# A retention layer and an MLP on one core: where the decay of the queries is multiplied in

## The chip, the cores and the metric

The kernel runs on one core of a Trainium2 chip. TensorE (PE) multiplies matrices and writes PSUM; VectorE (DVE) and ScalarE (ACT) empty PSUM, cast and combine; GpSimd (POOL) and SyncE (SP) issue transfers here. The metric is the device time of one execution in microseconds (us), lower is better.

## The reference

A retention layer (attention without softmax, with a decay per head) over batch 8, 8 heads, 576 positions, head size 64, and then a two-matrix MLP with a leaky rectifier on the 4608 tokens of 512 features. Cut to what matters:

```python
scores = (1 / sqrt(64)) * q @ k.T
gamma = 1 - 2 ** (-5 - arange(8))                 # one per head
Dmat = where(i >= j, gamma ** (i - j), 0)         # position i looks back at j
x = ((scores * Dmat) @ v), heads side by side     # 4608 x 512
h = x @ w_in                                      # w_in 512 x 2048
out = maximum(0.01 * h, h) @ w_out                # w_out 2048 x 512
```

`gamma ** (i - j)` splits into a factor of the query's position and one of the key's position. The kernel multiplies v by the key's factor.

## The kernel before, in words

**Units and groups.** The tokens are cut into 36 units u of 128 rows, each two chunks of 64 positions of one sequence (a sequence is 9 chunks, so some units span two). Four units make one group g of 512 tokens for the MLP; there are nine groups. Decays are counted inside blocks of 256 positions, four chunks; `place(c)` is a chunk's number in its block, 0 to 3.

**Jobs of a unit** (names as in the lists of orders):

- `ld u.1`, `ld u.0`, `ld u.2` load k, q and v in float32 (line 346). Units 0 to 11 come through POOL's queue (k0 and q0 through SP's), later ones through SP for k and q and POOL for v. Each of the three has four buffers, so the load of unit u waits for the cast of unit u - 4.
- `ck u`, `cq u`, `cv u` write 16-bit copies. `ck` is a plain cast (line 371). `cq` multiplies q by the query's factor and the scale, `cv` multiplies v by the key's factor; on VectorE that is one product with a table from the constants `cs` (line 375), on ScalarE eight small ones, one per head (line 381).
- `tp u.x` and `yt u.x` transpose k and q on TensorE and copy the result out of PSUM (units 0 to 7); `tr u` does it by one transposing transfer on SP's queue (from unit 8).
- `sb u` sums k and v into the running state (PSUM `sc`), `st u.j` adds it to the state kept in float32 on VectorE, `sx` casts that state to 16 bits. At a block's end `st` also multiplies by gamma to the 256th.
- `ca u` (or `sa u` in the first four units) multiplies k with q in PSUM `sc`, `mk u` applies the causal mask on VectorE, `ow u` (or `oa u`) multiplies by v and adds the state's part in PSUM `ot`.
- `x u` copies `ot` to the 16-bit tile `xT` (line 591), which the MLP reads. `ot` has two slots, so `ow` of unit u + 2 waits for `x u`.

**The MLP.** For groups 0 and 1 the first layer is plain: `h g.f.t` are blocks of matmuls of feature tiles from f on and tokens from t on, `l ...` the rectifier on ScalarE. The blocks of group 0 are cut by unit where that lets them start early: `h0.4.0` and `h0.6.0` need x0 and x1, `h0.4.256` needs x2, `h0.4.384` needs x3, and `h0.8.0` to `h0.15.0` need all four. `wi0` to `wi3` load the four quarters of w_in, `wo0` to `wo3` those of w_out. From group 2 on the first layer (`a g.n`), and in all groups the second (`b g`), is a scheme of seven products in place of eight: products p1 to p7 on TensorE (four matmuls of 256 columns in `a`, two halves of eight in `b`), copies `cA`, `u2`, `k5` out of PSUM on either engine, sums `22` and `12` on VectorE, results `11` and `21`. `xs` and `m` are the sums of its operands on VectorE; `wm` and `ws` are those of the weights, made once.

**The order.** Nothing is scheduled by a tool at build time: one list, `ORDER`, names every job, and each engine runs its own in that list's order; an engine whose next job has to wait holds all that stand behind it. `ENGINE` says which of VectorE and ScalarE runs a job that both can do. `+n@p` puts n idle matmuls of 512 columns (fillers) on TensorE; `@p` names one of four PSUM banks (`acc`). The beginning of TensorE's part of the list before:

```
+13 tp1.0 tp0.0 tp0.1 sb0 +4 tp1.1 sa0 +3 sb1 tp2.1 +2 sa1 tp2.0 oa0 +7 sa2 sb2 oa1 +2 tp3.1 h0.6.0 +2
tp3.0 h0.4.0 sa3 oa2 sb3 tp4.1 h0.4.256 oa3 tp4.0 tp5.0 h0.11.0 h0.9.0 h0.10.0 tp5.1 ca4 sb4 h0.4.384
```

Of the kernel before, what the change touches and what calls it, by code (L numbers as in the profile page):

```python
# [33 lines left out]
class Plan:  # L34
# [52 lines left out]
    for eng, names in {  # L87
        "DVE": """
            ck0 cq0 sx0.0 yt0.0 cq1 sx0.1 cv1 cq2 sx1.0 yt2.1 ck3 cq3 yt3.1 cv3 sx2.1 yt3.0 cq4 cv4 x3 ck5 cq5
            cv5 yt5.1 cq6 sx5 cv6 cq7 ck7 cv7 yt7.0 b0.cA cv8 ck10 sx8.0 cv9 cq9 cq11 cq12 cv10 b1.cA cv13 ck15  # L90
            cv14 cq14 cv15 cq15 sx13.1 sx14 cq16 cv16 cv17 cq17 cq18 a2.3.k5 sx17.0 cv18 sx18 cq19 a3.1.u2 x17
            cv20 ck21 cq21 sx19 a3.2.k5 cq22 cv22 sx20 ck23 cv23 cq23 x20 cv24 cq25 sx23 a4.2.cA cv25 a4.2.u2
            cq26 cq27 cv27 sx25 a5.0.u2 a5.0.k5 cq28 cq29 cv29 ck30 cq30 cv30 ck31 cv31 cq32 sx30 cq33 ck33
            a6.0.cA cv33 cv34 ck34 cq35 cq34 a6.2.cA b5.u2 cv35 a6.3.u2 x32 a7.0.cA x33 a7.0.k5 b5.21 a7.1.cA
            b6.11 b6.u2 a7.3.cA a7.3.u2 a8.0.k5 b7.k5 a8.2.u2 a8.2.k5 b7.21 a8.3.u2 b8.21
        """,
        "ACT": """
            cv0 yt0.1 x0 ck1 ck2 yt1.1 yt1.0 cv2 yt2.0 x1 sx1.1 sx2.0 x2 sx3.0 ck4 sx3.1 yt4.1 yt4.0 ck6 sx4.1
            x4 yt5.0 x5 yt6.0 yt6.1 sx6 yt7.1 sx7 x7 x6 ck8 b0.11 cq8 ck9 b0.u2 cq10 b0.k5 cv11 ck12 sx9 x8 ck11
            cv12 sx10 cq13 b0.21 x9 ck13 sx11 b1.11 sx12 x10 b1.u2 x11 ck14 a2.0.cA b1.k5 a2.0.u2 a2.0.k5 x12  # L100
            a2.1.cA a2.1.u2 x13 a2.1.k5 ck16 ck17 sx15 a2.2.cA a2.2.u2 b1.21 a2.2.k5 sx16 x14 a2.3.cA x15
            a2.3.u2 ck18 b2.cA a3.0.cA b2.11 a3.0.u2 a3.0.k5 a3.1.cA cv19 b2.u2 x16 a3.1.k5 ck19 b2.k5 a3.2.cA
            ck20 cq20 a3.2.u2 cv21 b2.21 ck22 x18 a3.3.cA a3.3.u2 a3.3.k5 x19 b3.cA a4.0.cA b3.11 sx21 ck24
            a4.0.u2 a4.0.k5 cq24 a4.1.cA a4.1.u2 sx22.1 a4.1.k5 x21 b3.u2 ck25 b3.k5 ck26 sx24 a4.2.k5 x22 cv26
            a4.3.cA x23 a4.3.u2 a4.3.k5 ck27 b3.21 a5.0.cA b4.cA ck28 cv28 sx26.0 b4.11 x24 ck29 a5.1.cA a5.1.u2
            a5.1.k5 x25 sx27 sx28 b4.u2 a5.2.cA x26 sx29 b4.k5 a5.2.u2 a5.2.k5 x27 a5.3.cA ck32 a5.3.u2 cv32
            a5.3.k5 cq31 b4.21 x28 x29 sx31.1 a6.0.u2 a6.0.k5 sx32 b5.cA a6.1.cA b5.11 a6.1.u2 x30 a6.1.k5 x31
            a6.2.u2 a6.2.k5 sx33 b5.k5 ck35 a6.3.cA a6.3.k5 sx34 sx35.0 a7.0.u2 b6.cA a7.1.u2 a7.1.k5 a7.2.cA
            a7.2.u2 b6.k5 a7.2.k5 x34 x35 a7.3.k5 a8.0.cA b6.21 a8.0.u2 b7.cA b7.11 a8.1.cA b7.u2 a8.1.k5
            a8.1.u2 a8.2.cA a8.3.cA a8.3.k5 b8.cA b8.u2 b8.k5 b8.11x so8.11x b8.11y  # L110
# [6 lines left out]
    ld0.1 ld0.2 ld0.0 ld1.0 ld1.1 ld2.1 ck0 ld2.0 cq0 ld1.2 cv0 cq1 ld2.2 +13@3 tp1.0@0 wi1 tp0.0@1 tp0.1@2 sb0 +4@3  # L117
    yt0.1 ld3.1 st0.0 ck1 yt0.0 ld3.0 cq2 yt1.0 tp1.1@3 ck2 sa0 +3@1 cv1 ld4.1 yt1.1 st0.1 sx0.0 sb1 tp2.1@2 +2@0
    mk0 ld3.2 sx0.1 cv2 sa1 tp2.0@1 ld4.0 st1.0 oa0 +7@0 mk1 sx1.0 st1.1s x0 yt2.1 yt2.0 sx1.1 sa2 sb2 oa1 +2@0
    ld5.0 x1 ck3 wi2 st2.0 tp3.1@0 mk2 h0.6.0@3 +2@1 ld4.2 st2.1 ck4 cq3 l0.6.0 yt3.1 tp3.0@2 ld5.1 sx2.0 h0.4.0@1  # L120
    yt3.0 cv3 ld5.2 sa3 oa2 cq4 sb3 wi3 x2 tp4.1@3 st3.0 mk3 l0.4.0 wi0 h0.4.256@0 sx3.0 sx2.1 cq5 ld6.0 oa3
    l0.4.256 tp4.0@2 x3 tp5.0@1 yt4.0 st3.1s ld6.1 h0.11.0@0 sx3.1 yt5.0 ld6.2 h0.9.0@2 yt4.1 ck5 cv4 ld7.0
    h0.10.0@1 l0.9.0 tp5.1@3 ld7.2 l0.10.0 ca4 sb4 h0.4.384@2 mk4 ld7.1 cv5 h0.8.0@1 l0.4.384 st4.1 ld8.2 yt5.1 ow4
    sb5 x4 h0.15.0@2 st5.0 sx4.1 st5.1 l0.11.0 h0.14.0@3 sx5 ld8.1 ca5 l0.14.0 cq6 l0.8.0 ld9.2 ws3.1 h0.13.0@0 mk5
    ld9.1 h0.0.128@3 l0.13.0 cv6 wo2 h0.0.384@1 l0.0.128 ld10.2 l0.15.0 tp6.0@0 h0.0.256@3 ck6 yt6.0 ld10.1 tp6.1@2
    l0.0.384 ow5 sb6 wo0 x5 h0.12.0@0 st6.0s yt6.1 ld8.0 h1.0.0@1 cv7 l0.0.256 cq7 ld9.0 h1.2.0@2 l1.0.0 ck7 st6.1
    ld10.0 tp7.0@3 h1.8.0@1 yt7.0 wo1 m0.0.0 h1.12.0@3 l1.8.0 ws3.0 sx6 ck8 ca6 sb7 l1.12.0 ld11.2 h0.0.0@1 st7.0
    l1.2.0 cv8 ck9 h1.4.0@3 mk6 ld12.2 l0.12.0 st7.1 h1.14.0@2 l0.0.0 cv9 wo3 l1.4.0 m0.1.0 tp7.1@0 sx7 sb8 h1.6.0@1
    st8.0s yt7.1 ow6 ca7 h1.10.0@3 ld11.1 x6 mk7 l1.14.0 wm2.0 ow7 sb9 ld13.2 m0.2.0 x7 b0.p1.0@0 l1.6.0 wm0.0
    h1.12.256@2 l1.10.0 cv10 ld11.0 wm1.0 h1.2.256@1 m0.0.1 h1.8.256@3 l1.2.256 m0.1.1 ld14.2 l1.12.256 h1.14.256@1  # L130
    sx8.0 l1.8.256 st9.0 ck10 b0.p1.1 l1.14.256 ws1.1 cq8 m0.2.1 h1.10.256@2 b0.cA@3 h1.0.256@1 ws1.0 b0.p6.0 st9.1
    l1.0.256 wm2.1 l1.10.256 h1.4.256@1 wm0.1 sx9 tr8 ld12.1 b0.p5.0@2 wm1.1 ld12.0 m0.3.1 b0.p5.1 cq9 b0.p6.1 ws2.1
    b0.k5 m0.3.0 b0.p2.0 b0.u2 cv11 sb10 ca8 b0.p7.0 mk8 tr9 ld13.1 st10.0 b0.p3.0 ck11 st10.1s ld15.2 cq10 ld13.0
    b0.p7.1 cq11 b0.p3.1 b0.22 b0.p2.1 l1.4.256 b0.12 wm3.0 ow8 ca9 sb11 wm3.1 cv12 b0.p4.0 tr10 ws4.1 b0.p4.1 mk9
    tr11 st11.0 ck12 b1.p1.0@1 ld16.2 ws2.0 ck13 st11.1 b1.p1.1 x8 m1.0.0 b0.21 h1.6.256@2 cq12 sx10 so0.1 b1.cA@3
    ow9 l1.6.256 ca10 ws4.0 sb12 sx11 b1.p2.0 m1.1.0 x9 tr12 ld14.0 st12.0 b1.p2.1 cq13 mk10 ld14.1 st12.1s b1.p6.0
    ld15.1 m1.0.1 ow10 b0.11 ca11 m1.2.0 a2.0.p1.0@2 b1.11 so0.0 b1.p5.0@0 m1.1.1 a2.0.cA@1 cv13 x10 b1.p5.1 mk11
    sx12 ld17.2 b1.p6.1 m1.2.1 m1.3.0 ow11 b1.u2 sb13 ca12 m1.3.1 a2.0.p2.0 x11 b1.p7.0 tr13 ld15.0 a2.0.11 xs2.0
    cq14 b1.k5 ld16.0 a2.0.p5.0@2 st13.1 b1.p7.1 a2.0.k5 xs2.1 ld17.0 mk12 a2.0.p6.0 xs2.2 b1.p3.0 a2.0.u2 sx13.1
    ck15 ck14 ld16.1 xs2.3 a2.0.p7.0 a2.0.p3.0 a2.0.22 b1.p3.1 a2.0.12 l2.0.22 a2.0.p4.0 b1.22 l2.0.12 a2.1.p1.0@2  # L140
    cv14 a2.0.21 b1.p4.0 b1.12 ld18.2 a2.1.p5.0@1 cq15 sb14 a2.1.k5 ow12 ca13 tr14 a2.1.cA@0 b1.p4.1 st14.0 x12
# [910 lines left out]
```

## Time and profile before

| what | value |
|---|---|
| median of 3 runs | 279.2 us (279.14 to 279.57) |
| profiled execution, its time | 279.54 us |
| its span, first to last instruction | 277.7 us |
| POOL busy | 72.4 us (26% of the span) |
| HBM read, written | 36.81 MB, 9.44 MB: 167 GB/s over the span |

The profile is one execution. Its page gives for each engine the busy time, its share of the span and the number of instructions; PEld is TensorE's weight load, which overlaps its matmuls. Rows of tenths cut the span into 40 slices of about 7 us. A row of waits reads: who waited, for whom, microseconds in total, how often, the longest. A row of the timeline reads: start, length, engine, line, operation, out<-in, shape, count, and in brackets how long the engine was idle before it and what ended that. A row of the groups by line reads: line, engine, operation, out<-in, shapes, count | busy us, mean ns of one | idle us before them and what ended it. A row of a window reads: from:to, length, then busy us of PE, PEld, DVE, ACT and POOL, the granted clock and the share of the DMA engines. A row of DMA issues ends with the size and the median us from issue to landing.

### The profile page before, as it was taken

To read this page: it belongs to the slowest core of one execution; us is meant where nothing else is said; L and a number is where in the kernel's file an instruction comes from. 1 tells how busy PE (TensorE), PEld (TensorE's weight loads), DVE (VectorE), ACT (ScalarE), POOL (GpSimd) and SP (SyncE) were. 2 spreads that over 40 slices of the span, in tenths; PEclk is the share of its full clock that TensorE was granted. 3 is DMA by queue.
4 is the path that set the end of the run, shared out by engine and by line. 5 is a ranking of instruction groups with operands and counts; after the bars stand their busy time and mean duration, and the time that the engine had idled before them with its cause. 6 is when DMAs were issued, how large, how long until landed. Compare 5 with 4: busy or idle time off the path is not lost.

```text
span 277.7 us, 10117 instructions
## 1 busy us (share of the span) xinstructions
PE 268.1 (97%) x4337; PEld 224.4 (81%) x4337; DVE 229.8 (83%) x431; ACT 206.7 (74%) x459; POOL 72.4 (26%) x92
## 2 busy tenths in 40 slices
PE   6878999999999999999999999999999999999994
...
DMA  7999999997899999799999998799041100300123
GB/s 219 224 240 238 293 287 269 277 216 177 208 256 220 220 295 227 173 236 230 257 222 255 183 228 183 170 247 219 20 139 74 44 2 2 153 0 0 78 97 132
DMA packets 94364, 50.04 MB, mean 180 GB/s; under 512 B 83312, under 2 KB 88560, under 8 KB 94320
## 3 DMA queue, kind: packets, MB, share of 16 engines
...
q8 instruction: 34, 0.56, 0.8%
q10 hardware_dynamic: 432, 0.24, 0.3%
q14 instruction: 10, 0.08, 0.1%
HBM read 36.81 MB, written 9.44 MB: 167 GB/s over the span
## 4 chain that ended last, share of the span: by engine, by line
PE 91%; DMA 5%; POOL 1%; ACT 1%; issue 1%; DVE 1%; POOLq 0%
PE acc L911 39%; PE acc L833 32%; PE acc L640 10%; DMA t<-in_k_dram 5%; PE ot L542 5%; PE sc L454 2%; PE sc L445 2%; PE sc L911 1%; POOL t L346 1%; PE acc L411 1%; DVE s L487 0%; POOL w_in L612 0%; ACT st L503 0%; DVE qk L375 0%; DVE s L460 0%
## 5 line engine op out<-in xcount | busy, mean ns | idle before, releaser
L911 PEld LDWEIGHTS <-gt 128*128 128x128 f16 x720 | 69.8, 98 | 8.4
L346 POOL DMA_DIRECT2D t<-in_v_dram x40 | 34.2, 857 | 100.5 <-DVE v L375 64.0
L911 PE MATMUL acc<-w_out,gt 128*128 128x256 f16 x416 | 51.5, 273 | 0.0
L833 PEld LDWEIGHTS <-w_in 128*128 128x128 f16 x448 | 42.4, 98 | 5.6
L853 ACT ACTIVATE gt<-acc 128x512 f16<-128x512 f32 x56 | 33.4, 599 | 16.6 <-PE acc L833 16.4
L861 ACT ACTIVATE gt<-sum 128x512 f16<-128x512 f32 x56 | 34.8, 633 | 4.7 <-DVE sum L857 4.7
L911 PE MATMUL acc<-w_mix,gt 128*128 128x256 f16 x288 | 36.2, 273 | 0.0
L833 PEld LDWEIGHTS <-w_sum 128*128 128x128 f16 x336 | 32.2, 98 | 4.1
L833 PE MATMUL acc<-xs,w_sum 128*128 128x256 f16 x224 | 33.6, 273 | 0.0
L833 PE MATMUL acc<-xT,w_in 128*128 128x256 f16 x224 | 33.5, 273 | 0.0
L833 PE MATMUL acc<-xs,w_in 128*128 128x256 f16 x224 | 33.4, 273 | 0.0
...
L640 PE MATMUL acc<-xT,w_in 128*128 128x256 f16 (+2 forms) x272 | 30.8, 266 | 0.7 <-ACT qkT L418 0.4
L911 PEld LDWEIGHTS <-mix 128*128 128x128 f16 x288 | 28.1, 98 | 3.3
L460 DVE TENSOR_TENSOR s<-sc,cs 128x512 f16<-128x512 f32 x36 | 24.6, 684 | 4.4 <-PE sc L445 2.3
L640 PEld LDWEIGHTS <-w_in 128*128 128x128 f16 x272 | 22.0, 98 | 5.8 <-issue 0.9
L857 DVE TENSOR_TENSOR sum<-acc,k 128x512 f32<-128x512 f32 x28 | 19.2, 686 | 7.9 <-PE acc L833 5.7
L647 ACT ACTIVATE gt<-acc 128x512 f16<-128x512 f32 x32 | 18.2, 601 | 6.3 <-PE acc L640 6.2
L786 ACT COPY k<-acc 128x512 f32<-128x512 f32 x29 | 17.0, 588 | 7.5 <-PE acc L833 3.7
L375 DVE TENSOR_TENSOR qk<-t,cs 128x512 f16<-128x512 f32 x30 | 20.5, 684 | 2.3 <-DMA t<-in_q_dram 2.3
L591 ACT CAST xT<-ot 128x512 f16<-128x512 f32 x31 | 18.2, 588 | 4.6 <-PE ot L542 4.6
L381 ACT ACTIVATE v<-t,cs 128x64 f16<-128x64 f32 x72 | 18.3, 343 | 4.1 <-DMA t<-in_v_dram 3.4
...
## 6 DMA issues: line engine op xcount, KB each, us to landing
t<-in_v_dram POOLq DMA_DIRECT2D x32, 256.0 KB, 5.1
out_dram<-osb POOLq DMA_DIRECT2D x16, 512.0 KB, 4.5
t<-in_k_dram SPq DMA_DIRECT2D x22, 256.0 KB, 4.8
t<-in_q_dram SPq DMA_DIRECT2D x22, 256.0 KB, 5.0
t<-in_q_dram POOLq DMA_DIRECT2D x10, 256.0 KB, 8.5
t<-in_k_dram POOLq DMA_DIRECT2D x10, 256.0 KB, 6.5
w_in<-in_moe_w_in_dram POOLq DMA_DIRECT2D x4, 512.0 KB, 7.8
w_out<-in_moe_w_out_dram POOLq DMA_DIRECT2D x4, 512.0 KB, 9.7
```

The source lines that it names most:

```text
L346: engine[eng].dma_start(out=t[CH * j : CH * j + rows], in_=(q, k, v)[x][b, :, CH * w : CH * w + rows, :].rearrange("h t d -> t h d"),)
L375: engine[e].tensor_tensor(out=view[0](out), in0=view[1](t32[u, 2 * x][:]), in1=view[1](decay(u, x)), op=MUL)
L381: nc.scalar.mul(out=out[:, at(h), :], in_=t32[u, 2 * x][:, h, :], mul=tab_sb[:, w, x, h : h + 1])
L460: landed[u] = nc.vector.tensor_tensor(out=s[:], in0=sc[:, :, 0], in1=mask_sb.unsqueeze(1).unsqueeze(1).to_broadcast([P, 2, NP, CH]), op=MUL,)
L591: moved[u] = copies[xe](out=x_of(u).rearrange("q c (j t) -> q j c t", j=2), in_=at)
L640: nc.tensor.matmul(out=a[:, n, :], lhsT=w_in16[:, c, (f0 + n) * P : (f0 + n + 1) * P], rhs=x[:, c, t0 : t0 + nt], start=(n == 0 and c == 0 ...
L647: nc.scalar.activation(out=y[:, f0 : f0 + nf, t0 : t0 + nt], in_=a[:], func=mybir.ActivationFunctionType.Lrelu)
L833: nc.tensor.matmul(out=r[:, f, :], lhsT=w[:, c, (2 * n + f) * P : (2 * n + f + 1) * P], rhs=rhs[:, c, :], start=fresh and c == 0 and f == ...
L853: w = op(what, "ACT", lambda: nc.scalar.activation(out=to(), in_=r[:], func=lr), after, [y], [r])
L857: what, "DVE", lambda: nc.vector.tensor_tensor(out=s[:], in0=r[:], in1=plus[:], op=ADD),
L861: f"l{g}.{n}.{what}", "ACT", lambda: nc.scalar.activation(out=to(), in_=s[:], func=lr), [j], [y],
L911: nc.tensor.matmul(out=(r[tb] if isinstance(r, tuple) else r)[:, tb, :], lhsT=lhs[n]()[:, f, tb * P : (tb + 1) * P], rhs=rhs[n][:, f, :], ...
```

## The change

`cq` becomes a plain cast like `ck`. The query's factor and the scale are multiplied in later: `x u`, now always on VectorE, multiplies `ot` by a table `q_tab` as it writes `xT`. In `ot` the positions lie along the columns, so the table holds, for each of the four places, a factor for each head and position. It is made in the kernel by four new VectorE jobs `tb0` to `tb3`, each a product of a fine and a coarse vector from the constants. The constants `cs` go from 148 to 236 columns of float32 per partition. `idle`, what the fillers read, is now a part of `w_mix` in place of a tile of its own; `s32` gets a pool of three buffers in place of four, and the state's product at a block's end is made in place. All jobs but the loads, stores and transfers stand in a new order, and `ENGINE` deals the copies and casts out anew: of the jobs that either engine can run, 61 go from VectorE to ScalarE and 38 the other way, apart from x.

```diff
-            scaled(t[:, 0], 0, qe, lambda h: 2 * (h % NP) + h // NP, (by_half, in_halves))
...
+        def plain(x, e):
+            copies[e](out=by_half(t[:, x]), in_=in_halves(t32[u, x][:]))
...
+        cast[u, 0] = add(f"cq{u}", qe, lambda: plain(0, qe), [loaded[u, 0]], [t], [t32[u, 0]])
...
+    def q_table():
+        for a in range(NB):
+            def run(a=a):
+                nb = CH // FINE
+                nc.vector.tensor_tensor(
+                    out=q_tab[:, a].rearrange("p c (b r) -> p c b r", b=nb),
+                    in0=fine_sb.unsqueeze(2).to_broadcast([P, NP, nb, FINE]),
+                    in1=coarse_sb[:, :, a].unsqueeze(3).to_broadcast([P, NP, nb, FINE]), op=MUL,
+                )
+
+            steep.append(add(f"tb{a}", "DVE", run))
...
     def outer_copy(u, j):
-        xe = by(f"x{u}", "ACT")
+        p0, p1 = place(2 * u), place(2 * u + 1)
 
         def cp():
             at = ot[:, :: -1 if u % 2 else 1, u % 2]
-            moved[u] = copies[xe](out=x_of(u).rearrange("q c (j t) -> q j c t", j=2), in_=at)
+            by_place = (
+                q_tab[:, p0 : p0 + 1].to_broadcast([P, 2, NP, CH]) if p0 == p1
+                else q_tab[:, p0 : p1 + 1 : p1 - p0] if p0 < p1
+                else q_tab[:, p0 : (p1 - 1 if p1 else None) : p1 - p0]
+            )
+            moved[u] = nc.vector.tensor_tensor(
+                out=x_of(u).rearrange("q c (j t) -> q j c t", j=2), in0=at, in1=by_place, op=MUL
+            )
```

The beginning of the list after, engine by engine:

```
TensorE: +13 tp0.1 +4 tp0.0 sb0 +3 tp1.0 sa0 tp1.1 +2 tp2.1 tp2.0 sa1 sb1 oa0 +7 +2 sa2 sb2 oa1 h0.4.0 +2 tp3.1 tp3.0
  oa2 sa3 sb3 tp4.1 h0.4.256 tp4.0 oa3 h0.6.0 h0.4.384 tp5.0 h0.9.0 h0.10.0 sb4 ca4 h0.8.0 h0.11.0
VectorE: tb2 cv0 tb0 cq1 st0.0 ck1 sx0.0 yt1.0 mk0 st0.1 cv1 sx0.1 tb1 tb3 st1.0 mk1 st1.1s x0 st2.0 st2.1 x1 ck3
  sx2.0 mk2 yt3.0 cv3 x2 st3.0 mk3 x3 st3.1s
ScalarE: ck0 cq0 yt0.1 yt0.0 ck2 cq2 yt1.1 yt2.0 yt2.1 cv2 sx1.0 sx1.1 cq3 yt3.1 ck4 l0.4.0 sx2.1 cq4 yt4.1 sx3.0 cq5
```

More of the change, by code (lines that the diff above doesn't have):

```diff
@@ L65 @@
     ap=4,
+    fp=3,
     cp=5,
@@ L88 @@
         "DVE": """
[L89 to L93, printed above, removed]
@@ L94 @@
-            a6.0.cA cv33 cv34 ck34 cq35 cq34 a6.2.cA b5.u2 cv35 a6.3.u2 x32 a7.0.cA x33 a7.0.k5 b5.21 a7.1.cA
-            b6.11 b6.u2 a7.3.cA a7.3.u2 a8.0.k5 b7.k5 a8.2.u2 a8.2.k5 b7.21 a8.3.u2 b8.21
+            cv0 cq1 ck1 sx0.0 yt1.0 cv1 sx0.1 ck3 sx2.0 yt3.0 cv3 sx3.1 cv4 ck5 cv5 sx4.1 ck6 cv6 cq7 ck7 sx6 cv7
+            cv8 cv9 cv10 b0.cA cq11 cv11 sx10 cv12 cq14 cv16 ck16 cv15 sx14 cv18 cq18 cv17 sx16 cq20 cv19 sx17.0
+            ck20 ck21 sx18 cq21 cv22 sx20 cv21 sx21 cq25 cv23 cv24 b3.u2 ck25 cv25 sx23 a4.2.u2 a4.2.k5 ck27 sx24
@@ L96 @@
+            cq27 cv27 cv28 cv29 cq29 sx27 sx28 cv30 ck30 ck31 cv31 cq31 sx29 cq33 cv35 a6.0.k5 cv33 sx31.1 a6.2.u2
+            cv34 a6.3.k5 a7.0.cA b5.21 a7.0.u2 ck35 sx34 b6.11 a7.3.u2 a8.1.cA a8.2.u2 a8.3.k5 b7.21 b8.k5 b8.21
         """,
         "ACT": """
-            cv0 yt0.1 x0 ck1 ck2 yt1.1 yt1.0 cv2 yt2.0 x1 sx1.1 sx2.0 x2 sx3.0 ck4 sx3.1 yt4.1 yt4.0 ck6 sx4.1
-            x4 yt5.0 x5 yt6.0 yt6.1 sx6 yt7.1 sx7 x7 x6 ck8 b0.11 cq8 ck9 b0.u2 cq10 b0.k5 cv11 ck12 sx9 x8 ck11
-            cv12 sx10 cq13 b0.21 x9 ck13 sx11 b1.11 sx12 x10 b1.u2 x11 ck14 a2.0.cA b1.k5 a2.0.u2 a2.0.k5 x12
@@ L101 @@
[L101 to L110, printed above, removed]
+            ck0 cq0 yt0.1 yt0.0 ck2 cq2 yt1.1 yt2.0 yt2.1 cv2 sx1.0 sx1.1 cq3 yt3.1 ck4 sx2.1 cq4 yt4.1 sx3.0 cq5
@@ L116 @@
 ORDER = """
[L117 to L141, printed above, removed]
@@ L207 @@
-    a8.3.p3.0 m8.0.0 a8.3.p2.0 a8.3.12 a8.3.p7.0 a8.3.11 b8.p5.0 a8.3.22 b7.21 b8.p1.0@0,1 l8.3.22 m8.1.0 l8.3.12
-    so7.1 b8.p1.1 m8.0.1 a8.3.p4.0 b8.cA@3 m8.1.1 b8.p5.1 a8.3.21 m8.2.1 b8.p6.0 m8.3.1 b8.p6.1 m8.2.0 m8.3.0
-    b8.p2.0 b8.u2 b8.k5 b8.11x so8.11x b8.p7.0 b8.p7.1 b8.p3.0 b8.22 b8.p3.1 so8.22 b8.p4.0 b8.12 b8.p4.1 so8.12
-    b8.p2.1 b8.21 so8.21 b8.11y so8.11y
+    tb2 ld0.1 ld0.2 ld0.0 cv0 ck0 ld1.0 ld1.1 ld2.1 ld2.0 ld1.2 ld2.2 cq0 tb0 +13@1 cq1 wi1 tp0.1@0 +4@2 tp0.0@1
+    ld3.1 sb0 st0.0 ld3.0 yt0.1 yt0.0 ck1 +3@3 ld4.1 tp1.0@1 sa0 sx0.0 yt1.0 tp1.1@3 mk0 ck2 st0.1 cv1 +2@2 cq2
@@ new lines @@
+    sx0.1 ld3.2 tb1 tp2.1@2 tp2.0@0 yt1.1 yt2.0 yt2.1 sa1 tb3 sb1 st1.0 mk1 cv2 oa0 sx1.0 ld4.0 +7@1 +2@3 st1.1s x0
+    sx1.1 ld5.0 sa2 sb2 wi2 st2.0 cq3 st2.1 oa1 x1 h0.4.0@2 +2@3 ck3 ld4.2 sx2.0 tp3.1@1 mk2 tp3.0@3 yt3.1 yt3.0 ck4
+    oa2 sa3 cv3 ld5.1 l0.4.0 sb3 x2 tp4.1@2 sx2.1 h0.4.256@3 st3.0 cq4 yt4.1 sx3.0 ld5.2 mk3 tp4.0@1 oa3 x3 h0.6.0@0
+    wi3 cq5 st3.1s wi0 ld6.0 ld6.1 sx3.1 yt4.0 l0.6.0 h0.4.384@1 tp5.0@2 ld6.2 h0.9.0@0 l0.4.384 yt5.0 cv4 h0.10.0@1
+    sb4 ca4 l0.4.256 ld7.0 ld7.2 ck5 l0.9.0 h0.8.0@3 st4.1 ld7.1 mk4 h0.11.0@0 ld8.2 cv5 ld8.1 ow4 l0.8.0 sb5
```

225 lines of the change are left out of this document (132 added, 93 removed), and 12 rows, old and new, of the table loads.

## The prediction

> **What bounds the kernel now.** I read the page first, then the waits of TensorE, then the timeline of the first 30 us, then the groups by line.
>
> ```profile
> span 277.7 us, 10117 instructions
> PE 268.1 (97%) x4337; PEld 224.4 (81%) x4337; DVE 229.8 (83%) x431; ACT 206.7 (74%) x459; POOL 72.4 (26%) x92
> PE   6878999999999999999999999999999999999994
> DMA  7999999997899999799999998799041100300123
> PE acc L411 <- DVE qk L375: 2.2, 2, 2.0
> PE acc L411 <- DVE qk L371: 1.3, 1, 1.3
> 60.00:200.00 140.00, 140.00 (x2576) 120.60 (x2577) 132.72 (x254) 125.63 (x294) 26.89 (x33) 1.00 0.99 213
> ```
>
> TensorE is the bound. It has idle tenths only in the first four slices and in the last. A busy TensorE need not be at its peak, but the timeline further down shows 32 matmuls of 256 columns from 50.13 to 53.62, 3.49 us, 0.109 us each, and I find that pace everywhere behind the head. From 60 to 200 us it is busy 140.00 of 140.00 us; VectorE (fifth number, 132.72) stands at 95% and ScalarE (125.63) at 90%. The change alters no matmul and leaves 33 fillers as they were. So the time can move in three places only: the head, where TensorE waits (the two longest rows of its waits are there), the middle, if VectorE falls behind, and the tail.
>
> The head is set by transfers and by the order of the work around them:
>
> ```profile
> 16.04 0.60 PE L980 MATMUL acc<-idle 128*128 128x512 f16 x2
> 16.80 0.89 POOL L346 DMA_DIRECT2D t<-in_q_dram  x1 [3.03 <-DMA w_in<-in_moe_w_in_dram]
> 17.23 0.68 DVE L371 CAST qk<-t 128x512 f16<-128x512 f32 x1 [2.23 <-DMA t<-in_k_dram]
> 17.97 0.40 PE L411 MATMUL acc<-ident,qk 128*128 128x128 f16 x4 [1.33 <-DVE qk L371]
> 24.46 0.69 DVE L591 CAST xT<-ot 128x512 f16<-128x512 f32 x1 [0.52 <-PE ot L542]
> 25.30 2.75 PE L640 MATMUL acc<-xT,w_in 128*128 128x512 f16 x12 [0.41 <-ACT qkT L418]
> 7.56 0.78 POOL L612 DMA_DIRECT2D w_in<-in_moe_w_in_dram  x1
> w_in<-in_moe_w_in_dram POOLq DMA_DIRECT2D x1, 512.0 KB, 8.7
> 9.20 0.91 POOL L346 DMA_DIRECT2D t<-in_q_dram  x1
> t<-in_q_dram POOLq DMA_DIRECT2D x1, 256.0 KB, 9.3
> 11.52 0.89 POOL L346 DMA_DIRECT2D t<-in_v_dram  x1
> t<-in_v_dram POOLq DMA_DIRECT2D x1, 256.0 KB, 8.1
> 17.68 0.77 POOL L612 DMA_DIRECT2D w_in<-in_moe_w_in_dram  x1
> w_in<-in_moe_w_in_dram POOLq DMA_DIRECT2D x1, 512.0 KB, 6.8
> ```
>
> Issue plus time to landing gives the gates: the first quarter of w_in (wi1) lands at 7.56 + 8.7 = 16.3, k3 just before 17.23, q3 at 9.20 + 9.3 = 18.5, v3 at 11.52 + 8.1 = 19.6, the second quarter (wi2) at 17.68 + 6.8 = 24.5. Between 16.64 and 17.97 TensorE stands still, though wi1 is there at 16.3: its next entry is tp3.1, which needs the cast of k3. And the first full-width block, h0.11.0, starts at 25.30, just behind the eviction x3 (24.46 + 0.69 = 25.15), while its weights came at 24.5.
>
> **The change part by part.** Prices:
>
> ```profile
> L375 DVE TENSOR_TENSOR qk<-t,cs 128x512 f16<-128x512 f32 x30 | 20.5, 684 | 2.3 <-DMA t<-in_q_dram 2.3
> L381 ACT ACTIVATE qk<-t,cs 128x64 f16<-128x64 f32 x48 | 12.2, 345 | 0.0
> L371 ACT CAST qk<-t 128x512 f16<-128x512 f32 x24 | 14.8, 622 | 2.3 <-DMA t<-in_k_dram 2.3
> L371 DVE CAST qk<-t 128x512 f16<-128x512 f32 x12 | 5.5, 466 | 5.0 <-DMA t<-in_k_dram 5.0
> L591 ACT CAST xT<-ot 128x512 f16<-128x512 f32 x31 | 18.2, 588 | 4.6 <-PE ot L542 4.6
> L591 DVE CAST xT<-ot 128x512 f16<-128x512 f32 x5 | 3.4, 685 | 0.5 <-PE ot L542 0.5
> L460 DVE TENSOR_TENSOR s<-sc,cs 128x512 f16<-128x512 f32 x36 | 24.6, 684 | 4.4 <-PE sc L445 2.3 <-PE sc L454 2.0
> L783 DVE COPY u<-acc 128x512 f32<-128x512 f32 x9 | 6.2, 686 | 2.7 <-PE acc L833 2.7
> cs<-ret_consts ACTq DMA_DIRECT2D x1, 74.0 KB, 3.0
> 6.10 2.02 ACT L381 ACTIVATE v<-t,cs 128x64 f16<-128x64 f32 x8 [2.97 <-DMA t<-in_v_dram]
> ```
>
> *The cast of q.* VectorE gives up 30 scalings of 0.684 us (20.5) and ScalarE 6 sets of eight (12.2). In their place stand 12 casts on VectorE at 0.466 (5.6) and 24 on ScalarE at 0.622 (14.9). VectorE -14.9, ScalarE +2.7.
>
> *The eviction x.* 31 leave ScalarE (-18.2); all 36 are on VectorE as a product of PSUM with a table in SBUF. The trace has that very form in L460 (sc times the mask), 0.684 us, as much as the plain VectorE copy (0.685), so I take 36 x 0.684 = 24.6 for the 3.4 of before, +21.2. The multiplication is free; the engine is what changes.
>
> *Moves to even this out.* By the two lists, ck on VectorE +1, cv +3, yt -4, sx +5, copies of the seven-product sets (cA, u2, k5) -10 at 0.686. With ScalarE's side at its own rows this comes to VectorE -4.0, ScalarE -1.4.
>
> *The tables.* Four products of 256 columns, each like the 0.42 us row at 14.25 below: VectorE +1.7. tb2 stands at the front of VectorE's queue and waits for cs; behind it are cv0, tb0, cq1. cs grows from 148 to 236 columns (74 to 118 KB): its landing, 1.15 + 3.0, moves between nothing and 3.0 x 118/74 = 4.8, to 5.95 at the latest, still ahead of v0, for which cv0 waits until 6.10. tb2 is hidden behind that wait; tb0 delays cq1 by 0.34. Bound for the other loads: 44 KB more at some 220 GB/s, 0 to 0.2 us; I take 0.1.
>
> Sum: VectorE -14.9 + 21.2 - 4.0 + 1.7 = +4.0 (1.4% of the span), ScalarE +2.7 - 18.2 - 1.4 = -17. Neither is on the path as a sum; their places are.
>
> *Queues.* Read engine by engine, SP's and POOL's lists are the same, entry by entry, before and after; every load, store and transpose keeps its place. The casts that free the load buffers come no later in the head, so landings stay.
>
> *Fillers.* Same 33 fillers, in the same groups but one of 4 and one of 3 changed about; `idle` is now a piece of w_mix, written by the same memset. Nothing.
>
> *The head, step by step.* TensorE's new order from oa1 on is h0.4.0, two fillers, tp3.1, tp3.0, oa2, sa3, sb3, tp4.1, h0.4.256, tp4.0, oa3, h0.6.0, h0.4.384, tp5.0, h0.9.0. x1 comes out at about 15.4 (oa1 needs sx1.0, behind cv2 of 2.0 us on ScalarE; earlier than wi1 in any case). h0.4.0 starts when wi1 has landed, 16.35, and takes 8 x 0.109 = 0.87; fillers to 17.65; tp3.1 follows the cast of k3 at 17.9. tp3.0 needs cq3, now 0.62 on ScalarE after q3 (18.5): 19.2. This is the new wait, 1.1 us; behind cq3 on ScalarE stand yt3.1, ck4 and l0.4.0, done by 20.7, and tp4.1, which wants the bank that l0.4.0 frees, comes at 20.95. oa2 19.45; sa3 after yt3.0 (0.42) 20.15; cv3 0.68 on VectorE to 20.7, sb3 20.8; x2 on VectorE to 21.3, h0.4.256 21.4 to 22.25; tp4.0; oa3 22.5, done 23.2; x3 to 23.95 (before: 25.15); h0.6.0 meanwhile, to 23.87; h0.4.384 24.0 to 24.9; tp5.0; h0.9.0 at 25.1, with wi2 there since 24.5. So at the first full-width block TensorE is 25.3 - 25.1 = 0.2 earlier and has one block more behind it, 0.87. Gain 1.05; I take 1.0 with the larger cs. Ends: 24.55 in place of 25.1 (wi2's landing) gives 1.6; another 1.05 us lost in the chain of eight waits gives 0.
>
> *Given back at a later gate?* The next weights are the nearest.
>
> ```profile
> 50.13 3.66 PE L640 MATMUL acc<-xT,w_in 128*128 128x256 f16 x32
> 53.62 1.04 PE L911 MATMUL acc<-w_out,gt 128*128 128x256 f16 x8
> 41.56 0.78 POOL L621 DMA_DIRECT2D w_out<-in_moe_w_out_dram  x1
> w_out<-in_moe_w_out_dram POOLq DMA_DIRECT2D x1, 512.0 KB, 10.3
> 14.25 0.42 DVE L491 TENSOR_TENSOR s<-stmp,cs 128x256 f32<-128x256 f32 x1
> 14.59 0.42 DVE L418 COPY qkT<-acc 128x512 f16<-128x512 f16 x1
> 265.56 0.69 DVE L887 TENSOR_TENSOR gt<-gt,mix 128x1024 f16<-128x1024 f16 x1
> 266.17 0.69 DVE L887 TENSOR_TENSOR gt<-gt 128x1024 f16<-128x1024 f16 x1
> ```
>
> b0.p1.1 needs the quarter wo1, landed at 41.56 + 10.3 = 51.9, and starts at 53.62: up to 1.7 us of gain pass.
>
> *The middle.* Back to back, VectorE instructions of 0.69 start 0.61 apart and those of 0.42 start 0.34 apart (last rows). The tightest place that I find in the new lists is from a4.0.22 to a4.3.22: 39 entries on VectorE, 27 x 0.60 + 11 x 0.334 + 0.68 = 20.55 us. TensorE has between a4.0.p7.0 and a4.3.p4.0, which wants a4.3.22, 23 products of four matmuls and 9 halves of eight (164 x 0.109 = 17.9) and 13 short retention entries at some 0.2 to 0.25, together 20.6 to 21.1. Cost 0 to 0.3 us; I take 0. From 60 to 200 us VectorE goes from 132.7 to about 135 of 140.
>
> *The tail.* The last products stand in the same order; a8.3.k5 and b8.k5 change engines with 2 us to spare. Nothing.
>
> The profiled execution took 279.54, its span is 277.7, 1.84 around it; the median of the runs is 279.2, 0.34 lower. 279.54 - 1.0 = 278.5 there, 278.2 as a median.
>
> **The rivals.** *VectorE becomes the bound in the middle (slower).* For it: 95% becomes 96.5%, x waits for ow in VectorE's own queue, and everything behind it with it. Against: no place above exceeds its TensorE work by over 0.3 us. It decides once the stalls sum to over 1.0, two late VectorE instructions of 0.6; five such give 3.0 - 1.0, 281.2, two to three 279.8 or so. Chance 0.14.
>
> *The gain in the head isn't there (no change).* If q3's cast or the chain of x2 and x3 runs 0.5 to 1.0 late, TensorE reaches h0.9.0 at 25.6 to 26.1 and 278.7 to 279.2 comes out. For it: eight hand-overs in 6 us. One way to this is POOL: in the row at 17.23 a VectorE cast took 0.68 us beside a POOL issue (16.80 to 17.69). Three more VectorE casts (cq1, ck1, sx0.0) now fall among the first issues; if POOL paid a cast's 0.466 for each, q3 would land 1.4 later, h0.9.0 start at 26.5, and 279.2 - 1.05 + 1.4 = 279.5 come out. Against: POOL itself waited 3.03 for a landing at 16.80, so issue has slack. Chance 0.22.
>
> That rule stands in the Trainium skill, "SBUF — State Buffer", section "Who interferes with whom": a VectorE cast in a two-port mode and GpSimd lock each other out for the whole instruction, whoever is first. By it the 279.5 just worked out could come about. Here VectorE was the one that waited, 0.68 for its usual 0.43 to 0.47; that POOL waits, the trace does not show.
>
> *The head gains more (277.6):* the chain keeps up with wi2. Chance 0.08.
>
> **How the numbers follow.** Gain of 0.6 to 1.4 in the head, 277.8 to 278.6: 0.56, the forecast, 278.2. A measurement here can tell 0.2%, 0.56 us. Faster: 0.56 + 0.08, less those that end just inside, 0.62; same 0.24; slower 0.14. The range goes from the larger gain with 0.2 of play, 277.4, to the first cases of a slow middle, 279.7, and leaves out some 0.15.
>
> **What would show it.** Right: matmuls with w_in at about 16.4; a wait of TensorE near 19 for ScalarE's cast; the first 512-column matmuls at about 25.1 with one more block behind them; VectorE at 233, ScalarE at 190 us busy; no TensorE wait between 60 and 270. Wrong: 512-column matmuls after 26, w_in landings that moved, or rows of TensorE waiting for VectorE (xT, sum) in the middle.

## The result: 8.4% slower, and TensorE waits for transfers

The changed kernel takes 302.8 us (300.4 to 304.9, four runs) against 279.2 us (278.9 to 279.6) on the same chip, a ratio of 1.084 [1.075, 1.094]. 278.2 was predicted, with 279.7 as the upper end. Its profiled execution took 304.9 us. Executions that lie over 1.5% above the fastest of their kernel are left out of the ratios in this document, but not out of its medians and ranges. Of the changed kernel's page, the span, the busy time, the tenths, the granted clock, the transfers by slice, two rows of the groups by line and three of issues:

```profile
span 303.1 us, 10042 instructions
...
PE 274.9 (91%) x4337; PEld 227.8 (75%) x4337; DVE 231.5 (76%) x443; ACT 192.0 (63%) x388; POOL 72.8 (24%) x92
...
PE   7688998915999989998999999699999999999995
...
PEclk9979999985999999999999999989999999999999
DMA  7999999999999999999979999989701110110123
GB/s 179 212 218 223 234 219 254 241 157 145 161 195 250 192 263 214 207 202 195 281 156 212 191 228 215 194 156 232 175 2 71 72 37 1 71 71 0 71 86 123
...
L361 POOL DMA_DIRECT2D t<-in_v_dram x40 | 34.4, 862 | 120.4 <-DVE v L404 97.2
...
L616 DVE TENSOR_TENSOR xT<-ot,q_tab 128x512 f16<-128x512 f32 x36 | 24.6, 684 | 2.3 <-PE ot L562 2.2
...
t<-in_v_dram POOLq DMA_DIRECT2D x32, 256.0 KB, 7.2
...
t<-in_k_dram SPq DMA_DIRECT2D x22, 256.0 KB, 6.4
t<-in_q_dram SPq DMA_DIRECT2D x22, 256.0 KB, 6.4
```

The engines do what was predicted: VectorE 231.5 us (233 predicted), ScalarE 192.0 (190), x 684 ns a row. TensorE's share falls from 97 to 91%. What has moved is the transfers: as many packets and bytes as before (94364, 50 MB), but from the first slice at a lower rate. The same rows of the page of before:

```profile
GB/s 219 224 240 238 293 287 269 277 216 177 208 256 220 220 295 227 173 236 230 257 222 255 183 228 183 170 247 219 20 139 74 44 2 2 153 0 0 78 97 132
...
L346 POOL DMA_DIRECT2D t<-in_v_dram x40 | 34.2, 857 | 100.5 <-DVE v L375 64.0
...
t<-in_v_dram POOLq DMA_DIRECT2D x32, 256.0 KB, 5.1
...
t<-in_k_dram SPq DMA_DIRECT2D x22, 256.0 KB, 4.8
t<-in_q_dram SPq DMA_DIRECT2D x22, 256.0 KB, 5.0
```

A load of k on SP's queue, alike in size and in place, takes 6.4 us from issue to landing in place of 4.8. TensorE's waits after, the first two rows, and its timeline around the first of them:

```profile
PE ot L562 <- DMA qkT<-qk: 9.3, 1, 9.3
PE acc L860 <- ACT gt L880: 2.6, 1, 2.6
```

```profile
61.68 0.32 PE L475 MATMUL sc<-v,qk 64*64 64x64 f16 x16
71.34 0.31 PE L562 MATMUL ot<-qkT,st 64*64 64x64 f16 x6 [9.35 <-DMA qkT<-qk]
```

From 62.00 to 71.34 TensorE stands and waits for tr8, the first transposing transfer. The job that waits is ca8. The length of tr8 stands, for the changed kernel, as a piece of the chain that ended last (start, length), and for the kernel before among the issues of the window from 56 to 60 us (the last number):

```profile
55.58 15.72 DMA qkT<-qk
```

```profile
DMA packets 1821, 0.77 MB, mean 192 GB/s; under 512 B 1738, under 2 KB 1738, under 8 KB 1821
...
q1 hardware_dynamic: 1706, 0.43, 63.8%
q0 software_dynamic: 115, 0.34, 27.1%
...
qkT<-qk SPq DMA_TRANSPOSE x1, 3.6
```

Issued at 55.58, tr8 lands at 71.3, 15.7 us later; before it was issued at 56.36 and took 3.6. Two questions follow. Why is every load slower? And why is this one transfer four times as slow?

The first had an answer that no profile shows, in the compiled program's addresses. The tiles lie one behind the other in each partition. The constants `cs` are 352 B longer, `q_tab` adds 4096 B, `idle` is 1024 B less: the tiles next behind them, the load buffers t32, move by 3424 B. They started at byte 75,776 of a partition before, a multiple of 512; after they start at 79,200, 96 B behind a multiple of 256. All tiles behind t32 start 96 B behind such a multiple as well.

### The profile page after: what moved, and what is told of

It reads as the page before. It is cut to its first block, busy times and chain, and to the rows that moved or that the text cites. A ratio compares the mean times of both kernels' runs of the same rounds, so it can differ in the third digit from the quotient of the medians.

```text
span 303.1 us, 10042 instructions
## 1 busy us (share of the span) xinstructions
PE 274.9 (91%) x4337; PEld 227.8 (75%) x4337; DVE 231.5 (76%) x443; ACT 192.0 (63%) x388; POOL 72.8 (24%) x92
## 2 busy tenths in 40 slices
DMA packets 94364, 50.09 MB, mean 165 GB/s; under 512 B 83312, under 2 KB 88560, under 8 KB 94320
## 4 chain that ended last, share of the span: by engine, by line
PE 61%; DMA 19%; DVE 9%; issue 4%; ACT 2%; POOL 1%; SPq 1%; ACTq 0%; DVEq 0%; POOLq 0%
PE acc L938 29%; PE acc L860 21%; DMA t<-in_v_dram 6%; DMA t<-in_q_dram 6%; DMA qkT<-qk 5%; PE acc L667 3%; PE ot L562 3%; DMA t<-in_k_dram 2%; DVE sum L884 2%; POOL t L361 1%; PE acc L1007 1%; PE sc L475 1%; SPq L361 1%; DVE v L404 1%; PE sc L938 1%
## 5 line engine op out<-in xcount | busy, mean ns | idle before, releaser
L938 PEld LDWEIGHTS <-gt 128*128 128x128 f16 x720 | 71.0, 99 | 9.2
L361 POOL DMA_DIRECT2D t<-in_v_dram x40 | 34.4, 862 | 120.4 <-DVE v L404 97.2
L938 PE MATMUL acc<-w_out,gt 128*128 128x256 f16 x416 | 52.3, 275 | 0.0
L880 ACT ACTIVATE gt<-acc 128x512 f16<-128x512 f32 x56 | 33.4, 598 | 16.5 <-PE acc L860 15.9
L400 ACT CAST qk<-t 128x512 f16<-128x512 f32 x47 | 28.3, 620 | 23.7 <-DMA t<-in_k_dram 13.4
L938 PE MATMUL acc<-w_mix,gt 128*128 128x256 f16 x288 | 36.9, 277 | 0.0
L667 PE MATMUL acc<-xT,w_in 128*128 128x256 f16 (+2 forms) x272 | 32.0, 269 | 2.6 <-issue 1.6
L813 ACT COPY k<-acc 128x512 f32<-128x512 f32 x32 | 18.6, 587 | 16.0 <-PE acc L938 11.4
L616 DVE TENSOR_TENSOR xT<-ot,q_tab 128x512 f16<-128x512 f32 x36 | 24.6, 684 | 2.3 <-PE ot L562 2.2
L884 DVE TENSOR_TENSOR sum<-acc,k 128x512 f32<-128x512 f32 x28 | 19.2, 685 | 8.7 <-PE acc L860 6.0
L404 DVE TENSOR_TENSOR v<-t,cs 128x512 f16<-128x512 f32 x30 | 20.4, 684 | 6.6 <-DMA t<-in_v_dram 5.2
L810 ACT COPY u<-acc 128x512 f32<-128x512 f32 x31 | 18.2, 587 | 10.5 <-PE acc L860 6.5
```

Of the source, the lines that this page charges most:

```text
L361: engine[eng].dma_start(out=t[CH * j : CH * j + rows], in_=(q, k, v)[x][b, :, CH * w : CH * w + rows, :].rearrange("h t d -> t h d"),)
L400: copies[e](out=by_half(t[:, x]), in_=in_halves(t32[u, x][:]))
L404: engine[ve].tensor_tensor(out=s[:], in0=t32[u, 2][:], in1=decay(u), op=MUL)
L616: moved[u] = nc.vector.tensor_tensor(out=x_of(u).rearrange("q c (j t) -> q j c t", j=2), in0=at, in1=by_place, op=MUL)
L667: nc.tensor.matmul(out=a[:, n, :], lhsT=w_in16[:, c, (f0 + n) * P : (f0 + n + 1) * P], rhs=x[:, c, t0 : t0 + nt], start=(n == 0 and c == 0 ...
L813: op("k5", ke, lambda: copies[ke](out=k5[:], in_=C[:]), [done["5"]], [k5], owned(C))
```

## Experiments

Names with a_ are the changed kernel, with b_ the kernel before. Each time is a median; the ratio behind it, with its 95% interval, is to the kernel before on the same chip (279.8 to 280.3 us). "Multiples of 512" are starts of tiles in bytes of a partition.

**1. The starts alone, in four kernels.** An unused tile is the only edit. a_start0:

```diff
     warm = const_pool.tile([P, 1], FP, name="warm")
+    pad = const_pool.tile([P, 40], FP, name="pad")
```

> The changed kernel with one unused tile of 160 B per partition behind warm. Nothing else is different: the same instructions in the same order on every engine. In the changed kernel every tile from t32 on starts 32 B behind a multiple of 64 B of a partition, in the kernel before on a multiple of 512 B; here it is a multiple of 512 B again. Theory A (the start of the tiles in a partition makes every transfer slower): 277.5 to 279.5 us, the predicted 278.2 among them, and the medians from issue to landing back at about 5 us for a load of k on SP's queue (6.4 in the changed kernel). Theory B (the new order, with tr8 and ca8 early and the casts on other engines, makes the waits): 299 to 306 us, landings as in the changed kernel. Theory C (VectorE's casts and its x rows hold up POOL's descriptors): 299 to 306 us as well.

288.6 us, 1.030 [1.025, 1.034]. More than half of the loss is gone with 160 unused bytes, but not all: the expected 277.5 to 279.5 was missed, and so was 299 of the rivals. A load of k on SP's queue lands in 5.1 us again, as theory A had it. a_start64 has 8 columns in place of 40:

> The changed kernel with an unused tile of 32 B behind warm: the tiles from t32 on start on a multiple of 128 B of a partition (64 too), but not of 256 B. Theory A in the form that a multiple of 64 B is enough: the time of the kernel whose tiles start on multiples of 512 B, within 0.5 us (277.5 to 279.5). Theory A in the form that 256 or 512 B is needed: 290 to 304 us. Theories B and C: 299 to 306 us.

304.6 us (298.7 to 306.7): no better than the changed kernel, and even its lowest time is above every one of a_start0; a multiple of 128 B is not enough. b_start352 puts 88 columns behind warm in the kernel before:

> The kernel before with an unused tile of 352 B per partition behind warm: every tile from t32 on starts 32 B behind a multiple of 64 B and 352 B behind a multiple of 512 B, as in the changed kernel; the order, the engines and the data are those of before. Theory A: slower than before by 15 to 30 us (294 to 309), a k load on SP's queue at 6.4 us from issue to landing (4.8 before). Theories B and C: 279.2 us within 0.3, landings as before.

291.4 us, 1.043 [1.038, 1.048]: the old order, arithmetic and data, and 11.6 us slower. Less than the 15 expected (a load of k on SP's queue takes 5.8 us, not 6.4), but neither rival allows any of it. b_w_start0 moves the weights:

> The kernel before with unused tiles of 288 B ahead of ident and 224 B behind warm: the weights w_in16, w_out16, w_mix and w_sum, which start 32 B behind a multiple of 64 B in the kernel before, start on a multiple of 256 B, and the tiles from t32 on still on a multiple of 512 B. Theory A: the weight loads land sooner than the 7.8 us (w_in) and 9.7 us (w_out) of before; 277.8 to 279.2 us, a gain only where the head waits for them. Theories B and C: 279.2 us within 0.3, landings as before.

279.9 us, 1.000 [0.998, 1.002]: no change. Whether the weights start on a multiple of 256 B, as here, or 224 B behind one, as in the kernel before, makes no difference.

The windows from 6 to 16 us, when little but loads and the first weights are under way, show the rate. After, a_start0, a_start64, in this order; a row is packets, MB, rate, and then the software queue's packets, MB and share:

```profile
DMA packets 1046, 2.22 MB, mean 222 GB/s; under 512 B 119, under 2 KB 631, under 8 KB 1046
...
q0 software_dynamic: 1046, 2.22, 108.6%
```

```profile
DMA packets 1222, 2.77 MB, mean 277 GB/s; under 512 B 165, under 2 KB 677, under 8 KB 1221
...
q0 software_dynamic: 1221, 2.75, 106.5%
```

```profile
DMA packets 1045, 2.24 MB, mean 224 GB/s; under 512 B 114, under 2 KB 626, under 8 KB 1045
...
q0 software_dynamic: 1045, 2.24, 108.9%
```

The transfer engines are busy all through in each of the three; the rate alone differs. By the single packets of the trace from 4 to 9 us, one of 4096 B (a load's) takes on average 199 ns before, 195 in a_start0, 302 after, 306 in a_start64 and b_start352. One of 1024 B (a weight's) takes 98 to 111 from 9 to 14 us in all of them. A load's row of a partition consists of eight pieces of 256 B, one per head, from eight places in memory; a weight's comes in longer rows. That only the short pieces suffer fits these numbers; no run changed the length of a piece.

The Trainium skill, "DMA: Bandwidth & Descriptors", section "How a descriptor splits into AXI transactions", says that a transaction has to start on a multiple of 256 B and that a read which doesn't pays for the bytes below its start. The page speaks of reads; here it is the written side that moves. If the rule held for writes too, a piece of 256 B that starts 96 B behind such a multiple would take 11 beats for 8, an estimate of 1.38 times the time. The packets measured 1.5 times, and as much at 128 B behind, where the rule would give 12 beats. The direction agrees, the size is the measurement's.

**2. 256 or 512, and which tiles.** a_start256 has 104 columns in the pad. b_loads352 moves the t32 buffers alone (a pad of 88 columns ahead of them, one of 40 behind); a_loads_start0 is its counterpart in the changed kernel, t32 alone put right.

> The changed kernel with an unused tile of 416 B behind warm: the tiles from t32 on start on a multiple of 256 B of a partition, but not of 512 B. If 256 B is what the transfers need: 286.5 to 291 us, as with multiples of 512 B (288.6). If 512 B is needed: 298 to 306 us, as with multiples of 128 B (304.6).

287.1 us, 1.022 [1.014, 1.030]: a multiple of 256 B does.

> The kernel before with the twelve t32 buffers alone 352 B behind a multiple of 512 B; all behind them (s32, st16, qk16, v16, qkT, osb and the rest) on multiples of 512 B again. Theory A1 (the loads into t32 are what slows): 289 to 293 us, nearly all of the 291.4 us of the kernel where everything is shifted, and loads of v on POOL's queue at 6.5 us. Theory A2 (the transposing transfers into qkT, or the results out of osb, are what slows): 279 to 281 us, loads at 5.1 us.

294.0 us, 1.048 [1.041, 1.056]: all of the 1.043 and just above the expected range, with every other tile on multiples of 512 B; v on POOL's queue at 6.9 us.

> The changed kernel with an unused tile of 160 B ahead of the t32 buffers and one of 352 B behind them: t32 starts on multiples of 512 B, everything behind it (st16, s32, qk16, qkT, osb and the rest) 352 B behind one, as in the changed kernel. Theory A1 (only the loads into t32 matter): 286 to 291 us, the 288.6 of the kernel where everything is on multiples of 512 B, and the first 13 us at over 240 GB/s. If the other tiles matter as well: 294 to 303 us.

289.1 us, 1.032 [1.025, 1.039], the 1.030 of a_start0; 277 GB/s from 6 to 16 us. So it is the loads into t32, and they alone, from both sides. This part is shown: it is worth 1.084 to 1.030 in the new order and 1.000 to 1.043 in the old.

**3. What is left, 1.030.** The longest row of TensorE's waits in a_start0, and the transfers from 58 to 66 us:

```profile
PE ot L563 <- DMA qkT<-qk: 8.0, 1, 8.0
```

```profile
GB/s 238 190 234 220 61 36 0 22 0 24 133 79 225 183 128 179 74 150 169 152 81 168 141 111 97 182 108 88 119 81 46 83 49 58 95 91 115 77 69 175
DMA packets 1364, 0.91 MB, mean 113 GB/s; under 512 B 1190, under 2 KB 1219, under 8 KB 1364
...
q1 hardware_dynamic: 1136, 0.28, 72.3%
q0 software_dynamic: 228, 0.62, 50.6%
```

tr8 again: issued at 51.55, landed 14.8 us later. This profiled execution, 292.6 us, is the longest of its kernel; in those of a_start256 (284.3 us) and a_loads_start0 (288.4 us) the wait for tr8 is 4.7 and 6.1 us. Its packets are 256 B (q1). In the window of before shown above they stood beside 115 packets of POOL's queue (q0) and 1706 of them got through in 4 us; here 1136 in 8 us beside 228. Before, tr8 is issued at 56.36, when POOL's backlog of loads and w_out quarters is just ending (its last landings are at 56.9 to 59.0), and lands at 60.0. In a_start0 a load that POOL issues at 52.81 lands 12.4 us later, at 65.2, and tr8 at 66.4: both times tr8 lands about 1 us behind the end of the backlog. In the new order the casts of unit 8 come sooner, tr8 goes out 4.8 us earlier, into the middle of the backlog, and ca8 stands sooner in TensorE's list. Two tries: a_ca8_later moves ca8 and mk8 behind most of the block b0, a_order_before keeps the arithmetic and takes the old order.

```diff
-... wm2.1 ld12.1 ca8 cq9 ... ck11 mk8 cq11 ... wm3.1 sb11 ow8
+... wm2.1 ld12.1 cq9 ... ck11 cq11 ... wm3.1 ca8 mk8 sb11 ow8
```

> The changed kernel with its tiles on multiples of 512 B (288.6 us), and in ORDER the products ca8 and the mask mk8 moved 28 places on for TensorE, from ahead of b0.p6.0 to ahead of sb11, so that the block b0 runs while the transposing transfer tr8 is under way (issued 51.55, landed 66.36 in the aligned kernel, where TensorE waits 8.2 us for it at 58.2). Theory D (what the alignment left is one stall: tr8 is issued into a backlog of POOL's loads, and the new order has ca8 ahead of the work that hid it): 279.5 to 282 us, no row of TensorE waiting over 2 us for qkT. Theory E (the 9 us left lie in VectorE's additional x rows and tables, wherever TensorE stands): 287 to 290 us, the wait reappears at another row.

283.9 us, 1.015 [1.008, 1.022]. The wait for tr8 is gone. The time lies between the two ranges, 2 us above theory D's: waits turn up elsewhere, as theory E had said. The longest, in TensorE's waits, and the reason in ScalarE's timeline:

```profile
PE acc L861 <- ACT acc L800: 2.6, 1, 2.6
```

```profile
116.40 0.59 ACT L881 ACTIVATE gt<-acc 128x512 f16<-128x512 f32 x1
120.39 1.14 ACT L401 CAST qk<-t 128x512 f16<-128x512 f32 x2 [3.40 <-DMA t<-in_k_dram]
```

ScalarE holds the evictions back because a cast ahead of them waits 3.4 us for k.

> The changed kernel's arithmetic (q only cast, x times q_tab on VectorE, tables tb0 to tb3, 118 KB of cs, idle in w_mix, three buffers for s32), tiles on multiples of 512 B, in the ORDER and with the engines of the kernel before; tb0 and tb1 stand behind cq1, tb2 and tb3 behind sb1. Theory D: tr8 goes out at about 56 us as in the kernel before and lands in 4 us; 278.5 to 282 us. Theory E: 285 to 290 us, with waits of TensorE for VectorE's x all over the middle.

287.2 us, 1.025 [1.020, 1.031]. In the old order tr8 takes 5.7 us and costs 0.8, but small waits are spread over the middle. Theory D fails here, and the time lies in theory E's range: in this order VectorE's additional work does cost, with 23% of the chain that ended last (1% in the kernel before). But VectorE is busy 241.3 us in it, 9.8 more than in the new order, which deals copies and casts to ScalarE. So the run does not tell what the new order loses.

**4. Late loads or VectorE?** a_loads_earlier repairs the two places that a_ca8_later showed.

```diff
-... mk20 tr21 a3.3.22 ...
+... mk20 ld23.1 ld24.1 tr21 a3.3.22 ...
```

> The changed kernel on multiples of 512 B with ca8 and mk8 ahead of b0.p3.1 (two blocks of TensorE sooner than in the last try, so that sb11 does not wait for mk8), and ld23.1 and ld24.1 ahead of tr21 on SP's queue: in the last try SP reached ld23.1 behind the transposing transfers and two other loads, the load landed at 119.9, and ScalarE's ck24 and ck23 (3.4 us of waiting) stood ahead of the evictions that TensorE waited 2.6 us for. Theory D, carried on (what is left is fixed places where the new order allows a load less time than it takes): the 2.6 and the 0.8 us go; 279 to 281.5 us, level with the kernel before. Theory E (VectorE's additional work costs the rest): 283 to 285 us, as in the last try, with the waits at other rows.

283.7 us, 1.017 [1.012, 1.022], from 280.2 to 285.9. The profiled execution is the best of them, 280.2, and both waits are gone in it, as theory D had it; but the median has not moved and lies in theory E's range. The next two start from this kernel. The first halves the loads, the second takes x from VectorE:

```diff
-  out=t[CH * j : CH * j + rows], in_=(q, k, v)[x][b, :, ...
+  out=t[CH * j : CH * j + rows, : H // 2 if u >= 12 else H], in_=(q, k, v)[x][b, : H // 2 if u >= 12 else H, ...
```

> The last kernel (starts on multiples of 512 B, ca8 later, ld23.1 and ld24.1 earlier; 283.7 us) with loads of half the size for units 12 to 35: heads 0 to 3 of q, k and v alone are loaded and the casts read them twice, so that every instruction of an engine stays and 72 loads bring 128 KB instead of 256 KB; the result is that of the first four heads' data. Theory D (the new order leaves a load too little time in places, and what is left comes from transfers that are late now and then): 278 to 280 us, and the runs within 1.5 us of one another (280.2 to 285.9 with whole loads). Theory E (VectorE's additional work): 282 to 285 us, runs as far apart as with whole loads.

280.5 us, 1.000 [0.997, 1.003]: level with the kernel before, with all work of the engines in place (VectorE is busy 231.1 us). It is below theory E's range and just above theory D's, and the runs still lie 4.9 us apart (278.1 to 282.9), where 1.5 was expected. The kernel before was not run with such loads; its TensorE, busy all through from 60 to 200 us, leaves it little to gain by them.

```diff
+            if u >= 12:
+                moved[u] = nc.scalar.copy(out=x_of(u).rearrange("q c (j t) -> q j c t", j=2), in_=at)
+                return
```

> The last kernel (283.7 us) with x of units 12 to 35 as a plain copy on ScalarE instead of the product with q_tab on VectorE; the decay of q is left out of these units. VectorE has 24 rows of 684 ns less (16.4 us), ScalarE 24 of about 590 ns more (14 us). Theory D: 282 to 286 us, no better. Theory E: 279 to 281 us.

287.9 us, 1.025 [1.018, 1.032], above both ranges. VectorE is busy 219.7 us for the 231.2 of a_loads_earlier, and the kernel is no faster; theory E's 279 to 281 does not come. By itself this is no clean test: x now stands in ScalarE's queue, where the order has no room for it (TensorE waits three times, 1.6 us in all, for ScalarE's xT). What speaks against theory E is a_half_loads.

**5. Is it the backlog that slows tr8?** The kernel of a_start0 with halved loads for units 7 to 13 alone; ca8 stays where the change put it.

> The changed kernel on multiples of 512 B (288.6 us; TensorE waits 4.7 to 8.2 us for tr8) with loads of half the size for units 7 to 13 alone: heads 0 to 3 of q, k and v are loaded and read twice by the casts, which leaves every instruction of an engine in its place. Theory F (tr8's packets take turns with those of a backlog on POOL's queue): tr8 lands within 8 us of its issue (13.0 to 14.8 with whole loads), the wait for it falls below 3 us, and the time to 281 to 285 us. If tr8 is slow at this place by itself: it lands 13 to 15 us behind its issue, wait and time as with whole loads, 285 to 290 us.

281.2 us, 1.004 [1.000, 1.007]. TensorE's waits, the row for tr8:

```profile
PE ot L578 <- DMA qkT<-qk: 1.5, 1, 1.5
```

tr8 lands 9.7 us behind its issue (8 was the bound expected; the w_out quarters are still in the backlog), the wait is 1.5 us for 4.7 to 8.0, and 1.030 becomes 1.004. So the backlog is what holds tr8 up. That tr8 is all of the 0.026 is not shown: a_ca8_later, in which the wait for it is gone, still stands at 1.015, and halved loads can help at other places too. That packets of two queues take turns on a transfer engine is my reading of the counts; it wasn't tried by itself.

**6. Do the two causes add?** a_ca8_later without the pad:

> The changed kernel with ca8 and mk8 moved on as in the last try, but without the unused tile: the tiles from t32 on start 32 B behind a multiple of 64 B again. If the two causes add: 302.8 less the stall of 9.3 us, and 283.9 plus some 12 us, so 294 to 298 us. If the stall at tr8 was nearly all that the start of the tiles costs the new order: 284 to 290 us.

304.5 us, 1.078 [1.069, 1.087]. Neither expectation. With slow loads, moving ca8 gains nothing: its wait is gone, and four others of 2.5 to 3.3 us take its place (a later transposing transfer, the sums of w_out, ScalarE at two places). The causes do not add; a slow load finds the next place with little slack.

## Why the prediction was wrong, point by point

*The step that failed* is *Queues*: "every load, store and transpose keeps its place ... so landings stay". The places did stay. The landings did not, for two reasons.

First, the price of a transfer was taken as fixed while the tile that it writes was moved. The step on the tables saw `cs` grow and priced it by its bytes, 0 to 0.2 us; in a_start0 those bytes cost nothing (cs lands in 3.0 us, as before). The 352 B by which it shifts the tiles behind it cost the most of all, 302.8 to 288.6. `q_tab` and the tile `idle` ("Nothing" under *Fillers*) moved them too, but by multiples of 256 B, which by part 2 do no harm.

Second, a place in one queue is not a time. tr8 kept its place on SP's queue, but its release (the casts of unit 8) and its user (ca8) moved against POOL's queue. The step on the middle bounded VectorE against TensorE and did not set a transfer against the work that hides it; its "I take 0" was therefore too small by what tr8 and the late loads cost, 1.030 to about 1.00.

*The head* was nearly right once the loads were. TensorE's timeline in a_start0, in which nothing but the starts is put right:

```profile
16.45 1.03 PE L668 MATMUL acc<-xT,w_in 128*128 128x256 f16 x8 [0.93 <-DVE xT L617]
...
19.42 0.40 PE L433 MATMUL acc<-ident,qk 128*128 128x128 f16 x4 [0.71 <-ACT qk L401]
...
25.43 1.89 PE L668 MATMUL acc<-xT,w_in 128*128 128x512 f16 x8
```

These are h0.4.0, tp3.0 behind its new wait for ScalarE's cast, and h0.9.0. The steps had 16.35, 19.2 with a wait of 1.1, and 25.1. One gate was another: h0.4.0 waits for x1, not for the weights. In a_loads_earlier, the first block with w_in, the longest gap and the first block of 512 columns:

```profile
15.88 1.03 PE L668 MATMUL acc<-xT,w_in 128*128 128x256 f16 x8 [0.93 <-DVE xT L617]
...
23.68 1.49 PE L668 MATMUL acc<-xT,w_in 128*128 128x256 f16 x20 [1.25 <-issue]
...
25.23 1.89 PE L668 MATMUL acc<-xT,w_in 128*128 128x512 f16 x8
```

Against 25.30 before, and with one more block of 0.87 us behind it, TensorE is 0.94 us ahead here (0.74 in a_start0); 1.0 was taken. That it comes so close is in part luck: h0.4.0 begins 0.47 us sooner than in the steps, and before 23.68 TensorE stands for 1.25 us that the steps did not have and for which the profile shows no reason. In the changed kernel the first and the last of these rows read

```profile
20.26 1.03 PE L667 MATMUL acc<-xT,w_in 128*128 128x256 f16 x8 [1.00 <-DVE xT L616]
...
28.98 1.89 PE L667 MATMUL acc<-xT,w_in 128*128 128x512 f16 x8
```

which is a sign named beforehand for a wrong prediction, 512-column matmuls after 26. Another came too: w_in's landings moved, from 7.8 to 9.9 us.

*VectorE.* The sum, +4.0 predicted, came to +1.7, ScalarE's -17 to -14.7; x at 684 ns is exact. With loads that come in time VectorE is not the bound in the middle: a_half_loads has all of its work and the time of the kernel before.

*The rivals.* None had a slower transfer in it. That VectorE's casts hold POOL up is not borne out: POOL's issue of v takes 862 ns for 857; its longer idle time, 120.4 us for 100.5, ends with the cast of v, which waits for slower loads.

*What is left of the change.* With t32 on multiples of 512 B, ca8 later and loads that come in time (a_half_loads), 1.000 [0.997, 1.003]: the 0.94 us of the head are not in the total. In the profiled execution of a_loads_earlier, one place in the middle that the kernel before doesn't have, near 95 us, takes as much:

```profile
PE sc L476 <- issue: 1.0, 1, 1.0
```

What holds TensorE there the profile does not show.

No version here beats the kernel before.
